# Two-branch mixer on one core: the first weight load split 1 to 3, x blocks loaded ahead of the q and k weights, one weight load held back, and new orders on all engines

## The chip, the core and the metric

One core of a Trainium2 chip runs the whole program. The metric is the device time of one execution in microseconds (us). The core has five engines that matter here: TensorE (PE, matrix products into PSUM banks), VectorE (DVE), ScalarE (ACT), GpSimd (POOL) and SyncE (SP). SP, ACT and POOL also issue DMAs, each in its own order; the DMAs all run on the same 16 DMA engines.

## What is computed

x has 2048 tokens of width 512, all data is bf16. xn is the layer norm of x (no gain or bias). Two branches work on xn, and the result is x + A + B.

```python
# A: 32 heads of 16; each token attends to itself and 7 earlier tokens, 2 apart
q, k, v = split(xn @ wqkv)
logits[s, w] = q[s] . k[s - 2*w] * 16**-0.5          # w = 0..7; before token 0: -1e9
A = (sum_w softmax(logits)[s, w] * v[s - 2*w]) @ wo
# B: gated MLP with mixing over tokens
z = gelu(xn @ w_in)                                   # 1792 columns: z1 | z2, 896 each
g = w_sp @ layernorm(z2) + b_sp                       # w_sp is 2048 x 2048
B = (z1 * g) @ w_out
```

## The kernel before

The program is first recorded as a list of named tasks, each with its engine, what it reads and writes, and (for a DMA) a channel. `Plan.add` (line 54) derives from that what each task waits for. `ORDERS` (line 206) then lists, written out by hand for each engine, the names of its tasks; `Plan.follow` (line 95) sets that order, and `Plan.emit` (line 117) writes each engine's instructions with the semaphore waits that the list of dependences asks for. Nothing reorders at run time: an engine that waits at a task holds all tasks listed behind it, SP's and POOL's DMA issues among them. So a task's place in `ORDERS` is as much a part of the kernel as what it does.

The 2048 tokens are 16 blocks of 128, in four groups of four. For block b the head of the program runs:

- `ldx{b}` (`ld_x`, line 525): the load of 128 KB of x into one of eight slots (slot b mod 8). x0, x1, x2 and x4 to x15 are issued by SP, x3 by ACT. A load into a slot used before waits until the block that had it has been normalised: x13 for norm5, x14 for norm6.
- `bnst`, `bnag` (DVE, lines 593 and 596): mean and variance; `rstd` (POOL, line 598): variance to the power of -0.5; `norm` (DVE, line 600): xn.
- The transpose to xnT. Blocks 0 to 3: `xTr` on PE (line 617), copied out of PSUM by `xTe` (ACT) and, for half of block 0, `xTf` (DVE). Blocks 4 to 15: `xTd`, a DMA transpose that SP issues (line 604).

Then PE makes, per block, `z2_{b}_0` and `z2_{b}_1` (`z_pair`, line 789; four matmuls of 448 columns each, PE line 799), `V{b}` (`v_pair`, line 637; four of 512 columns, PE line 644), and per group of four blocks `Q{j}_{c}` and `K{j}_{c}`, c = 0 to 3 (`qk_pair`, line 659; PE line 667). ACT takes them out of PSUM (`z2g`, `Ve`, `QKe`, `halo`). DVE forms the products of q and k for the logits (`prod`, line 692, and `padd`, line 696, 128 x 4096 elements each), PE sums them over a head (`lg`, line 705). V goes to a scratch tensor in DRAM (`Vw`, line 655) and is read back shifted. Later come the softmax, the `z1` products (needed from the end of the head on), the token mixing (`P1` to `P7`, PE line 922, with sums of w_sp and of z2 prepared by DVE), the gate and the output products (`out`, lines 1029 and 1033).

The weights of the head: `w_in2a` and `w_in2b` are the two 448-column halves of the z2 part of w_in, in four row chunks of 128. `ld_win_h` (line 535) loads each in two pieces of two chunks (224 KB each), the first issued by SP, the second by ACT. `ldq` and `ldk` (line 549, 512 KB each), `ldwv` (line 557, 512 KB) and `ldw_in1` (the z1 weights, 896 KB, line 531) are issued by SP. q, k and x4 to x7 wait for SP's piece of `w_in2a`:

```python
                512 * 512 * 2, ("wqk", which), reads=[("w_in2a", 0)],
...
        for b in range(4, 8):
            ld_x(b, "sp", after=[("w_in2a", 0)])
...
            if j == 1:
                ld_win("w_in1", 0, FH, "sp", after=[("xn", 2)])
```

SP's order begins `ldx0 ldx1 ldw_in2a_0 ldw_in2b_0 ldx2 ldx4 ldx5 ldq ldk ldx6 ldx7 ldx8 ldx10 ldx9 ldx11 ldw_in1 ldwv ldx12 xTd5 xTd7 ldx15 ldx14 xTd4`. DVE's order takes bnst5, 4, 7, 8 first after the statistics of blocks 0 to 3. POOL's order has the store `Vzero` (16 rows of zeros into the scratch tensor) behind rstd6.

Of the kernel before, what the change touches and what calls it, by code (L numbers as in the profile page):

```python
# [207 lines left out]
warm xTr0 fill0 z2_0_0 xTr1 z2_0_1 z2_1_0 xTr2 z2_1_1 xTr3 z2_2_0 z2_2_1 z2_3_0 Q0_0 z2_3_1 K0_0 K0_1 Q0_2 Q0_1
K0_2 K0_3 V0 V2 Q0_3 V1 V3 V4 V5 V7 Q1_0 K1_0 Q1_1 V6 Q1_3 K1_1 K1_3 K1_2 z2_4_0 Q1_2 z2_6_1 z2_4_1 z2_5_1
z2_5_0 z2_6_0 z2_7_1 z2_7_0 lg0_0 V11 V8 V9 V10 K2_0 K2_1 Q2_0 K2_2 Q2_1 Q2_2 K2_3 z2_8_1 Q2_3 z2_8_0 z2_9_0  # L210
z2_9_1 z2_10_0 z2_11_0 z2_11_1 lg1_0 z2_10_1 V13 V12 Q3_0 K3_0 Q3_1 V15 K3_1 V14 Q3_3 K3_3 z2_12_0 Q3_2 K3_2
z2_14_1 z2_12_1 z2_13_1 lg2_0 z2_13_0 z2_15_1 z2_15_0 z2_14_0 z1_0_0 z1_4_1 z1_0_1 z1_4_0 z1_2_0 z1_6_0 z1_10_0
z1_2_1 z1_10_1 z1_6_1 z1_8_1 z1_15_0 z1_15_1 z1_8_0 z1_12_1 z1_12_0 lg3_0 z1_9_1 z1_14_1 z1_9_0 z1_14_0 z1_13_0
z1_3_0 z1_13_1 z1_11_1 z1_11_0 z1_3_1 z1_7_1 z1_5_0 z1_5_1 z1_7_0 P1_0 z1_1_0 z1_1_1 P2_0 P5_0 P1_1 P6_0 P5_1
P3_0 P7_0 P6_1 P4_0 P2_1 P7_1 P1_2 P3_1 P4_1 P2_2 P1_3 P6_2 P5_2 P7_2 P3_2 P2_3 P5_3 P4_2 P6_3 out2_0 P7_3
out0_0 P1_4 P4_3 P3_3 P2_4 P6_4 P5_4 P7_4 out6_0 P1_5 P4_4 P3_4 P5_5 out4_0 out10_0 P2_5 P1_6 out8_0 P6_5 P5_6
P7_5 P3_5 P6_6 P4_5 out14_0 out12_0 P7_6 P2_6 P1_7 P3_6 out15_0 P4_6 P2_7 P6_7 out13_0 P7_7 P5_7 out11_0 P3_7
# [20 lines left out]
bnst4 bnst7 bnag4 bnst8 bnag8 bnst9 bnag7 bnag9 bnst10 bnst6 bnst11 norm4 bnag11 bnag6 norm5 norm7 prod0_0
bnag10 norm6 prod0_1 bnst12 zq0 norm11 prod0_2 padd0_1 bnag12 bnst15 norm10 norm8 bnst14 padd0_2 norm9 bnag15
bnag14 prod0_3 prod1_1 padd0_3 zv0 bnst13 norm15 prod1_0 norm14 prod1_2 bnag13 norm12 padd1_1 padd1_2 prod1_3  # L240
norm13 padd1_3 prod2_0 zq1 prod2_1 zv1 padd2_1 prod2_2 prod2_3 zq2 padd2_2 padd2_3 prod3_1 zv2 zn0 prod3_0
# [4 lines left out]
pvc2 sz3_1 srec1 pv14 u_8 pv12 S4_4 S13_5 pva2048_3 S2_5 pva1024_3 sattn1 h_4 pvc3 u_12 pv13 S4_5 S13_6 pv15
pva2048_4 u_15 pva1024_4 S2_6 pvc4 pv11 h_5 pv9 pva2048_5 S4_6 pva1024_5 S13_7 pvc5 pv5 S2_7 pv7 u_11 pva2048_6
h_6 pva1024_6 S4_7 pvc6 u_7 pv1 pv3 pva2048_7 pva1024_7 h_7 pvc7 u_1 u_3 fin1_1
""".split(),
    pool="""  # L250
ident0 mhalf rstd0 ident1 rstd1 rstd2 rstd3 ktpad mask0 mlog0 rstd5 mask1 rstd4 mlog1 rstd7 mlog2 rstd6 Vzero
rstd11 rstd10 rstd8 rstd9 rstd15 rstd12 rstd14 rstd13 zr0 zr1 ldbsp zr2 zr3 ldwo0 ldwo1 ldwout ldwo2 ldwo3
""".split(),
# [23 lines left out]
def build_kernel(nc, A_x, A_wqkv, A_wo, B_x, B_w_in, B_w_sp, B_b_sp, B_w_out, out,   # L277
# [82 lines left out]
    with ExitStack() as es:  # L360
# [164 lines left out]
        def ld_x(b, eng="sp", after=()):  # L525
            sl = b % 8
            dma(eng, lambda e: e.dma_start(xin_ap(sl), x2[128 * b:128 * b + 128, :]), 128 * 512 * 2,  # L527
                ("xin", sl), reads=after, writes=[("xin", sl)], name="ldx%d" % b)
# [650 lines left out]
```

## Time and profile before

| what | value |
|---|---|
| median of three runs | 228.82 us (228.8 to 229.11) |
| the profiled execution | 228.85 us, of it the span 227.1 us |
| granted TensorE clock | 1.0 |
| PE busy in the span | 97% |
| DVE busy in the span | 91% |
| ACT, POOL busy | 61%, 18% |

The span is the time from the first to the last instruction that the profile shows; the execution's own time has 1.75 us around it. A busy share of 97% says that there are some 6 us in which PE does nothing; where these lie, and what ends them, is asked of the waits and of the stretches. DVE is nearly as full, so that a gap on PE can also come from it.

### The profile page before, as it was taken

What the parts mean: (1) busy time and instruction counts of PE and PEld (TensorE: products, weight loads), DVE (VectorE), ACT (ScalarE), POOL (GpSimd) and SP (SyncE); (2) the same over time, 40 slices, a digit from 0 to 9 for tenths busy, and PEclk for the clock granted to TensorE, in tenths of its full rate; (3) what the DMA queues carried; (4) which work ended last, traced back from release to release, by engine and by line L of the source; (5) the groups of instructions that cost most, each with busy time, mean ns of one, the idle gap of its engine ahead of it and who ended that gap; (6) DMA issues with size and microseconds to landing.
All of it is one profiled execution on the core that took longest, in us unless ns stands there. A gap on an engine that the chain in (4) does not pass through costs nothing.

```text
span 227.1 us, 3077 instructions
## 1 busy us (share of the span) xinstructions
PE 220.9 (97%) x1142; PEld 115.6 (51%) x1142; DVE 207.3 (91%) x213; ACT 138.0 (61%) x247; POOL 39.9 (18%) x40
## 2 busy tenths in 40 slices
PE   7899799999999999999999999999999999999995
PEld 2454355455454676765555554454544544444443
DVE  4759999999999999999999999999999999999800
ACT  2579657988997898548547354345352546255651
POOL 2527929181320200201410000000000000000000
PEclk9999999999999999999999999999999999999999
DMA  6895464122964006855949669993899576378562
GB/s 204 258 360 130 116 179 102 26 69 45 222 172 118 0 0 208 99 111 136 248 123 213 139 169 227 192 226 73 170 197 211 156 157 140 115 156 179 155 150 69
DMA packets 84768, 34.18 MB, mean 151 GB/s; under 512 B 69281, under 2 KB 84401, under 8 KB 84753
## 3 DMA queue, kind: packets, MB, share of 16 engines
q1 hardware_dynamic: 74592, 23.90, 49.4%
q10 hardware_dynamic: 9280, 8.62, 13.2%
q0 software_dynamic: 880, 1.47, 2.1%
q8 instruction: 9, 0.15, 0.3%
q14 instruction: 7, 0.05, 0.1%
HBM read 12.98 MB, written 4.21 MB: 76 GB/s over the span
## 4 chain that ended last, share of the span: by engine, by line
PE 88%; DMA 5%; DVE 3%; SPq 2%; issue 0%; DVEq 0%
PE ps L922 37%; PE ps L799 19%; PE ps L1033 11%; PE ps L667 9%; PE ps L1029 6%; PE ps L644 5%; DMA arena<-in_A_x_dram 2%; DMA arena<-in_B_w_in_dram 2%; DVE fpool L593 2%; SPq L527 1%; DMA arena<-arena 1%; DVE arena L692 1%; PE ps L705 1%; DVE arena L600 0%; SPq L549 0%
## 5 line engine op out<-in xcount | busy, mean ns | idle before, releaser
L922 PE MATMUL ps<-arena 128*128 128x448 bf16 x448 | 86.5, 352 | 0.0
L922 PEld LDWEIGHTS ps<-arena 128*128 128x128 bf16 x448 | 43.8, 98 | 41.3
L799 PE MATMUL ps<-arena 128*128 128x448 bf16 x256 | 51.1, 353 | 0.5 <-DMA arena<-in_B_w_in_dram 0.5
L799 PEld LDWEIGHTS ps<-arena 128*128 128x128 bf16 x256 | 30.4, 121 | 18.9 <-issue 0.8
L992 DVE TENSOR_TENSOR arena<-arena 128x4096 bf16<-128x4096 bf16 x16 | 36.3, 2281 | 0.3
L692 DVE TENSOR_TENSOR arena<-arena 128x4096 bf16<-128x4096 bf16 x16 | 36.3, 2283 | 0.1
L810 ACT ACTIVATE arena<-ps 128x896 bf16<-128x896 f32 x32 | 28.4, 914 | 10.8 <-PE ps L799 10.8
L928 ACT ACTIVATE arena<-ps 128x448 bf16<-128x448 f32 x32 | 17.2, 540 | 25.7 <-PE ps L922 22.4
L667 PE MATMUL ps<-arena 128*128 128x512 bf16 x128 | 29.6, 379 | 0.0
L996 DVE TENSOR_TENSOR arena<-arena 128x4096 bf16<-128x4096 bf16 (+1 forms) x16 | 28.0, 1753 | 0.2
L598 POOL TENSOR_TENSOR fpool<-fpool 128x1 f32<-128x1 f32 x16 | 24.2, 1527 | 21.9 <-DVE fpool L596 21.9
L696 DVE TENSOR_TENSOR arena<-arena 128x4096 bf16<-128x4096 bf16 x12 | 27.4, 2286 | 0.1
L1033 PE MATMUL ps<-arena 128*128 128x512 bf16 (+2 forms) x119 | 27.0, 366 | 0.0
L667 PEld LDWEIGHTS ps<-arena 128*128 128x128 bf16 x128 | 14.5, 113 | 13.0
L675 ACT ACTIVATE arena<-ps 128x1024 bf16<-128x1024 f32 x16 | 16.1, 1027 | 6.1 <-PE ps L667 6.1
L1033 PEld LDWEIGHTS ps<-arena 128*128 128x128 bf16 x119 | 11.4, 98 | 12.8
L1042 ACT ACTIVATE arena<-ps 128x512 bf16<-128x512 f32 (+1 forms) x16 | 9.3, 589 | 13.1 <-PE ps L1033 12.9
L928 ACT ACTIVATE arena<-ps,fpool 128x448 bf16<-128x448 f32 x16 | 10.0, 630 | 11.8 <-PE ps L922 11.8
L644 PE MATMUL ps<-arena 128*128 128x512 bf16 x64 | 15.1, 379 | 1.6 <-DMA arena<-arena 1.6
L1029 PE MATMUL ps<-arena 128*128 128x512 bf16 (+2 forms) x68 | 16.6, 366 | 0.0
L818 ACT ACTIVATE arena<-arena 128x896 bf16<-128x896 bf16 x16 | 15.4, 960 | 0.1
L835 POOL TENSOR_TENSOR fpool<-fpool 128x4 f32<-128x4 f32 x4 | 9.0, 2258 | 33.8 <-DVE fpool L832 33.8
(71 smaller groups left out, 179.3 us busy)
## 6 DMA issues: line engine op xcount, KB each, us to landing
arena<-in_A_x_dram ACTq DMA_DIRECT2D x17, 128.0 KB, 2.4
vscr<-arena SPq DMA_DIRECT2D x16, 128.0 KB, 1.9
arena<-in_A_x_dram SPq DMA_DIRECT2D x15, 128.0 KB, 3.2
out_dram<-arena ACTq DMA_DIRECT2D x15, 128.0 KB, 2.2
arena<-in_A_wqkv_dram SPq DMA_DIRECT2D x3, 512.0 KB, 5.3
arena<-vscr ACTq DMA_DIRECT2D x6, 256.0 KB, 3.4
arena<-vscr ACTq DMA_DIRECT2D x1, 1152.0 KB, 6.2
arena<-vscr ACTq DMA_DIRECT2D x1, 1024.0 KB, 7.1
```

Source lines behind the costliest of these rows:

```text
L644: last = t.matmul(bank(k + i), AC(off["xnT"] + dc * S + 128 * (b + i), [[1, 128]]), AC(off["wv_raw"] + 512 * dc, [[1, 512]]), start=(dc == ...
L667: last = t.matmul(bank(k + which), AC(off["wqk"] + 1024 * dc + col0, [[4, 128]]), AC(off["xnT"] + dc * S + 512 * j, [[1, 512]]), start=(dc ...
L692: T("dve", lambda v: v.tensor_tensor(pbv, qb, kb, ALU.mult), reads=[("QT", c, j), ("KT", c, j), ("KTpad", c, j)], writes=[("pb", s_)], est ...
L696: T("dve", lambda v: v.tensor_tensor(A("pb", 4096, 4096 * a), A("pb", 4096, 4096 * a), A("pb", 4096, 4096 * b), ALU.add), reads=[("pb", b) ...
L799: last = t.matmul(bank(k + hf, HF), AC(off["xnT"] + dc * S + t0, [[ts, 128]]), AC(off["w_in"] + 1792 * dc + c0, [[1, HF]]), start=(dc == 0 ...
L810: T("act", lambda a: a.activation(A(nm, FH, FH * b).rearrange("p (t n) -> p t n", t=2), PC(512 * k, [[512, 2], [1, HF]]), ACTF.Gelu_apprx_ ...
L922: last = t.matmul(bank(k, HF), AC(lo + 128 * s, [[1, 128]]), mov(s), start=(first and s == 0), stop=(s == 7), skip_group_check=True)
L928: T("act", lambda a: a.activation(dst, bank(k, HF), ACTF.Identity, **kw), reads=[("ps", k), "bspf"], writes=[key], est=est, name="%s_%d" % ...
L992: T("dve", (lambda iv, tv, av: lambda v: v.tensor_tensor(tv, iv, av, ALU.mult))(iv, tv, av), reads=[("attn", pairs[i][b]) for b in blks] + ...
L996: T("dve", (lambda n: lambda v: v.tensor_tensor(AC(off["Vs"], [[4096, 2], [1, n]]), AC(off["Vs"], [[4096, 2], [1, n]]), AC(off["Vs"] + n, ...
L1029: t.matmul(po, AC(off["OT"] + 512 * os_ + 128 * cc, [[1, 128]]), AC(off["wo"] + 512 * cc + c0, [[1, n]]), start=False, stop=False, skip_gr ...
L1033: last = t.matmul(po, AC(off["uT"] + FH * us + 128 * fc, [[1, 128]]), AC(off["w_out"] + 512 * fc + c0, [[1, n]]), start=False, stop=(fc == ...
```

## The change

Four things are changed in the text of the kernel:

1. `ld_win_h` gets the place of its cut: `w_in2a` is dealt 1 chunk to SP (112 KB) and 3 to ACT (336 KB); `w_in2b` stays 2 and 2.
2. q, k and x4 to x7 wait for x1 and no longer for SP's piece of `w_in2a`. In SP's order x4, x5, x8, x6 and x7 stand ahead of q and k; `ldwv` now stands behind x10, x11, x9 and x13.
3. `w_in1` waits for the transpose of block 7, and stands behind `xTd11` in SP's order.
4. All five orders are new. The number and kind of instructions stay the same.

```diff
-        for nm, lo, hi, h0, h1 in (("w_in1", 0, FH, 0, 4), (("w_in2a", 0), FH, FH + HF, 0, 2),
-                                   (("w_in2a", 1), FH, FH + HF, 2, 4), (("w_in2b", 0), FH + HF, 2 * FH, 0, 2),
+        for nm, lo, hi, h0, h1 in (("w_in1", 0, FH, 0, 4), (("w_in2a", 0), FH, FH + HF, 0, 1),
+                                   (("w_in2a", 1), FH, FH + HF, 1, 4), (("w_in2b", 0), FH + HF, 2 * FH, 0, 2),
...
-        def ld_win_h(nm, lo, n):
-            for h in range(2):
+        def ld_win_h(nm, lo, n, cut):
+            for h, (c0, c1) in enumerate(((0, cut), (cut, 4))):
...
-        ld_win_h("w_in2a", FH, HF)
-        ld_win_h("w_in2b", FH + HF, HF)
+        ld_win_h("w_in2a", FH, HF, 1)
+        ld_win_h("w_in2b", FH + HF, HF, 2)
...
-                512 * 512 * 2, ("wqk", which), reads=[("w_in2a", 0)],
+                512 * 512 * 2, ("wqk", which), reads=[("xin", 1)],
...
-            ld_x(b, "sp", after=[("w_in2a", 0)])
+            ld_x(b, "sp", after=[("xin", 1)])
...
-            if j == 1:
-                ld_win("w_in1", 0, FH, "sp", after=[("xn", 2)])
             for b in bl:
                 ln_block(b)
+            if j == 1:
+                ld_win("w_in1", 0, FH, "sp", after=[("xnT", 7)])
```

The orders, as far as they belong to the head (the first tasks of each; the rest is permuted as well):

```diff
 pe:
-... z2_2_0 z2_2_1 z2_3_0 Q0_0 z2_3_1 K0_0 K0_1 Q0_2 Q0_1
-K0_2 K0_3 V0 V2 Q0_3 V1 V3 V4 V5 V7 Q1_0 K1_0 Q1_1 V6
+... z2_2_0 z2_2_1 z2_3_0 Q0_0 K0_0 K0_1 z2_3_1 Q0_1 Q0_3
+Q0_2 K0_2 V0 K0_3 V1 V3 V2 V7 V6 V4 K1_0 Q1_0 V5 Q1_1
 dve:
-... norm2 bnst5 norm3 bnag5 bnst4 bnst7 bnag4 bnst8 bnag8 bnst9 bnag7 bnag9 bnst10 bnst6 bnst11 norm4
-bnag11 bnag6 norm5 norm7 prod0_0 bnag10 norm6 prod0_1
+... norm2 bnst5 norm3 bnag5 bnst8 bnst7 bnst6 bnag6 bnst4 bnag7 bnag8 bnag4 bnst10 bnst11 norm5 bnst9
+norm6 prod0_0 norm7 bnst13 bnag10 bnag9 prod0_1 bnag13 zq0 norm4 padd0_1
 pool:
-ident0 mhalf rstd0 ident1 rstd1 rstd2 rstd3 ktpad mask0 mlog0 rstd5 mask1 rstd4 mlog1 rstd7 mlog2 rstd6 Vzero
-rstd11 rstd10 rstd8 rstd9
+ktpad ident0 mhalf Vzero ident1 rstd0 rstd1 rstd2 rstd3 rstd5 mask0 mlog0 mask1 mlog1 mlog2 rstd6 rstd7 rstd4
+rstd10 rstd9 rstd8 rstd15
 sp:
-ldx0 ldx1 ldw_in2a_0 ldw_in2b_0 ldx2 ldx4 ldx5 ldq ldk ldx6 ldx7 ldx8 ldx10 ldx9 ldx11 ldw_in1 ldwv ldx12 xTd5
-xTd7 ldx15 ldx14 xTd4 Vw0 xTd6
+ldx0 ldx1 ldw_in2a_0 ldw_in2b_0 ldx2 ldx4 ldx5 ldx8 ldx6 ldx7 ldq ldk ldx10 ldx11 ldx9 ldx13 ldwv ldx14 xTd5
+xTd6 xTd7 ldx15 xTd4 Vw1 Vw3 ldx12
```

More of the change, by code (lines that the diff above doesn't have):

```diff
@@ L207 @@
     pe="""
[L208 to L217, printed above, removed]
@@ L218 @@
-P4_7 out9_0 out7_0 out5_0 out3_0 out1_0 out1_1
+warm xTr0 fill0 z2_0_0 xTr1 z2_0_1 z2_1_0 xTr2 z2_1_1 xTr3 z2_2_0 z2_2_1 z2_3_0 Q0_0 K0_0 K0_1 z2_3_1 Q0_1 Q0_3
+Q0_2 K0_2 V0 K0_3 V1 V3 V2 V7 V6 V4 K1_0 Q1_0 V5 Q1_1 Q1_3 K1_1 Q1_2 K1_2 z2_4_1 z2_4_0 z2_5_0 K1_3 z2_7_0
+z2_5_1 z2_6_0 z2_6_1 z2_7_1 V9 V10 V8 lg0_0 Q2_0 K2_1 K2_0 V11 Q2_1 Q2_2 K2_3 K2_2 Q2_3 z2_8_1 z2_8_0 z2_9_0
+z2_10_1 z2_9_1 z2_10_0 z2_11_0 z2_11_1 lg1_0 V15 V12 V14 V13 K3_2 Q3_1 K3_1 Q3_2 K3_0 Q3_0 z2_13_0 z2_13_1
+z2_12_0 K3_3 z2_12_1 z1_0_0 Q3_3 lg2_0 z2_15_0 z1_0_1 z2_15_1 z2_14_1 z2_14_0 z1_4_0 z1_4_1 z1_6_1 z1_2_0 z1_6_0
@@ L237 @@
 steps0 steps1 zeros bnst0 bnag0 norm0 bnst1 bnag1 xTf0 norm1 bnst2 bnag2 bnst3 bnag3 norm2 bnst5 norm3 bnag5
[L238 to L241, printed above, removed]
@@ L247 @@
-pva2048_4 u_15 pva1024_4 S2_6 pvc4 pv11 h_5 pv9 pva2048_5 S4_6 pva1024_5 S13_7 pvc5 pv5 S2_7 pv7 u_11 pva2048_6
-h_6 pva1024_6 S4_7 pvc6 u_7 pv1 pv3 pva2048_7 pva1024_7 h_7 pvc7 u_1 u_3 fin1_1
+bnst8 bnst7 bnst6 bnag6 bnst4 bnag7 bnag8 bnag4 bnst10 bnst11 norm5 bnst9 norm6 prod0_0 norm7 bnst13 bnag10
+bnag9 prod0_1 bnag13 zq0 norm4 padd0_1 bnst15 norm10 prod0_2 bnag15 bnag11 norm9 padd0_2 bnst12 bnst14 prod0_3
+norm8 bnag14 norm11 padd0_3 prod1_0 zv0 bnag12 prod1_1 norm15 padd1_1 prod1_2 norm12 prod1_3 padd1_2 zq1 norm14
@@ L249 @@
+sattn1 u_8 S4_4 pva1024_2 S13_5 pvc2 S2_5 pv14 u_12 pv12 pva2048_3 S4_5 h_4 pva1024_3 pvc3 pv15 pv13 S13_6
+pva2048_4 S2_6 pva1024_4 h_5 S4_6 pvc4 pv11 u_15 pv9 S13_7 pva2048_5 pva1024_5 h_6 pvc5 u_11 pv5 S2_7 pv7
+pva2048_6 pva1024_6 pvc6 u_7 pv3 S4_7 pv1 pva2048_7 pva1024_7 h_7 pvc7 u_3 u_1 fin1_1
 """.split(),
     pool="""
-ident0 mhalf rstd0 ident1 rstd1 rstd2 rstd3 ktpad mask0 mlog0 rstd5 mask1 rstd4 mlog1 rstd7 mlog2 rstd6 Vzero
-rstd11 rstd10 rstd8 rstd9 rstd15 rstd12 rstd14 rstd13 zr0 zr1 ldbsp zr2 zr3 ldwo0 ldwo1 ldwout ldwo2 ldwo3
+ktpad ident0 mhalf Vzero ident1 rstd0 rstd1 rstd2 rstd3 rstd5 mask0 mlog0 mask1 mlog1 mlog2 rstd6 rstd7 rstd4
@@ L253 @@
+rstd10 rstd9 rstd8 rstd15 rstd11 rstd14 rstd12 rstd13 zr0 zr1 ldbsp zr2 zr3 ldwout ldwo0 ldwo1 ldwo2 ldwo3
 """.split(),
     sp="""
-ldx0 ldx1 ldw_in2a_0 ldw_in2b_0 ldx2 ldx4 ldx5 ldq ldk ldx6 ldx7 ldx8 ldx10 ldx9 ldx11 ldw_in1 ldwv ldx12 xTd5
-xTd7 ldx15 ldx14 xTd4 Vw0 xTd6 Vw2 Vw1 Vw4 Vw3 xTd10 ldx13 Vw5 xTd8 xTd9 xTd11 Vw7 Vw6 xTd15 xTd12 Vw8 xTd14
-xTd13 wT1_1 Vw9 Vw11 wT0_1 wT1_0 Vw13 Vw10 Vw15 Vw12 wT0_0 Vw14 lgT2 lgT0 lgT3 lgT1 wT2_0 wT2_1 wT3_0 wT3_1 OTd0
-uT_2 uT_0 uT_4 wT4_0 wT4_1 wT5_0 OTd1 uT_6 wT5_1 OTd2 uT_8 uT_10 wT6_0 wT6_1 OTd3 uT_12 uT_14 uT_13 wT7_0 wT7_1
@@ L259 @@
-OTd4 uT_15 uT_11 OTd5 OTd6 uT_9 uT_5 uT_7 OTd7 uT_3 uT_1 st1_0
+ldx0 ldx1 ldw_in2a_0 ldw_in2b_0 ldx2 ldx4 ldx5 ldx8 ldx6 ldx7 ldq ldk ldx10 ldx11 ldx9 ldx13 ldwv ldx14 xTd5
+xTd6 xTd7 ldx15 xTd4 Vw1 Vw3 ldx12 Vw0 Vw2 xTd9 Vw6 xTd8 Vw4 xTd10 Vw5 xTd11 ldw_in1 xTd15 Vw7 Vw9 xTd12 wT1_1
+xTd14 Vw8 xTd13 Vw11 Vw10 wT0_0 Vw14 wT0_1 Vw12 wT1_0 Vw15 Vw13 lgT0 lgT2 lgT1 lgT3 wT2_0 wT3_0 wT2_1 wT3_1
+wT4_0 OTd0 uT_0 uT_2 wT4_1 wT5_0 uT_4 OTd1 uT_6 wT5_1 wT6_0 uT_12 uT_10 uT_8 OTd2 wT6_1 wT7_0 wT7_1 uT_14 OTd3
@@ L260 @@
+uT_15 uT_13 OTd4 OTd5 uT_11 uT_9 uT_5 OTd6 uT_7 OTd7 uT_3 uT_1 st1_0
 """.split(),
```

53 lines of the change are left out of this document (30 added, 23 removed).

## The prediction

> **What bounds the kernel now.** I read the engine table first, then the stretches, then the waits, then the chain that ended last. The first two say which engine sets the end and where it is not full:
>
> ```profile
> PE 220.9 (97%) x1142; PEld 115.6 (51%) x1142; DVE 207.3 (91%) x213; ACT 138.0 (61%) x247; POOL 39.9 (18%) x40
> ```
>
> ```profile
> core 0: us, PE busy (x) PEld busy (x) DVE busy (x) ACT busy (x) POOL busy (x), PEclk, DMA share, GB/s
> ...
> 12.00:18.00 6.00, 6.00 (x31) 3.14 (x30) 4.32 (x11) 4.26 (x10) 1.46 (x4) 1.00 1.04 352
> 18.00:24.20 6.20, 6.18 (x29) 2.79 (x27) 6.20 (x11) 6.02 (x13) 5.82 (x5) 1.00 0.53 111
> 24.20:25.80 1.60, 0.05 (x1) 0.05 (x2) 1.60 (x4) 0.82 (x2) 1.60 (x2) 1.00 0.64 156
> 25.80:60.00 34.20, 34.20 (x177) 16.78 (x178) 34.06 (x30) 26.55 (x53) 16.26 (x6) 1.00 0.40 98
> ```
>
> Columns: stretch, length, then busy us of each engine. PE is full from 12 us on, except 24.20 to 25.80; from 25.8 to 224.8 it never waits, at granted clock 1.00. The change alters no matmul, so 199 us behind 25.8 are fixed unless an edit opens a gap there, and all that can be won are the gaps ahead. The waits name them:
>
> ```profile
> DVE fpool L593 <- DMA arena<-in_A_x_dram: 4.7, 3, 2.7
> ...
> PE ps L644 <- DMA arena<-arena: 1.6, 1, 1.6
> ```
>
> L644 is the V product; it waits once, 1.6 us, for the DMA transpose of a block (V4 for xnT 4). L593 is bn_stats; its longest wait, 2.7 us, is for an x block. The chain joins the two:
>
> ```profile
> 1.73 4.47 DMA arena<-in_B_w_in_dram
> 6.20 0.02 issue
> 6.22 0.34 SPq L527
> ...
> 8.65 4.97 DMA arena<-in_A_x_dram
> 13.62 0.02 issue
> 13.65 0.69 DVE fpool L593
> ...
> 23.15 2.56 DMA arena<-arena
> 25.71 0.04 issue
> 25.75 2.76 PE ps L644 x12
> ```
>
> First number: start. The SP half of the first z2 weights lands at 6.20; until then SP may not issue x4. Block 7, behind the 1 MB of q and k weights, lands at 13.62, and DVE, which takes it as its next block, stands still from 10.95. Everything behind it on DVE is late by that, down to norm6 (ends 21.48). SP's load of x14 waits for norm6, and the transpose of block 4 stands behind that load: issued at 23.15, landed at 25.71, V4 at 25.75.
>
> **The stall's size.** The V product before V4 starts at 23.16. Start to start a product of four 512-column matmuls takes 0.863, so V4 could start at 24.02: the stall is 25.75 - 24.02 = **1.73 us**.
>
> **The change, part by part.**
>
> *z2 weights 1 to 3.* SP's piece becomes 112 KB, ACT's 336 KB. In the trace ACT's half landed at 4.48, SP's at 6.20, though issued only 0.64 apart: in 2 to 6 us each queue moved some 170 KB/us, and SP had x0 and x1 in front. Now 368 KB (SP) stand against 336 KB (ACT), so both should be in by about 5.5 (estimate: at 170 KB/us each, with the 0.9 us from last packet to landing that the 6.20 shows). z2_0_0 started at 6.35; its other operands were ready at 5.96 (ACT's copy of block 0) and 6.10 (DVE's), so at most 0.15 is won there. It is not kept: PE next waits at 9.42 (0.31 of idle) for the transpose of block 2, set by norm2 (ends 9.37) and so by x2's landing at 7.33. x2 comes when nearly all 1408 KB of the head loads are through, which the dealing does not change. I take 0; the other bound is -0.31, if SP's 112 KB less bring x2 in 0.65 earlier. The Trainium skill, "DMA: Bandwidth & Descriptors", section "Issuing engines are not separate DMA queues", says that DMAs of all issuers interleave on the same 16 engines and that issuing from several saves only sequencer time. By it this edit is worth nothing (227.1); by the queue rates of the trace up to 0.3 (226.8).
>
> *x4 to x8 ahead of q and k, waiting for x1 and not for w_in2a.* x1 landed at 4.46, so SP issues x4 at 4.5 (was 6.22), then x5, x8, x6, x7 at steps of 0.47, q at 6.85 and k at 7.35 (were 7.08 and 7.55). The queue is then never empty. Blocks 6 to 11 landed 0.37 apart (128 KB, 346 KB/us); from x2's 7.33 that gives x7 at 9.2 (was 13.62), q at 10.7, k at 12.3. Upper bound: q's and k's old landings, 11.03 and 12.88, plus 384 KB more in front (1.1): 12.1 and 14.0. PE needs q at 12.90 (Q0_0) and k at 13.76 (K0_0): no cost, at the bound 0.24.
>
> *DVE's order.* Steps from the trace: bn_stats 0.60, bn_aggr 0.10, norm 0.31, a product 2.20. From 10.30 (end of bnag5's turn): bnst8, 7, 6, bnag6, bnst4, three bnag, to 13.1; bnst10, bnst11 to 14.3; norm5 ends at 14.7; bnst9; norm6 ends at 15.6; prod0_0 (was 18.80) to 17.8; norm7 ends at 18.2; bnst13, two bnag; prod0_1 18.9 to 21.1; bnag13, zq0; norm4 ends at 21.75. Against before: norm5 is 3.9 earlier, norm6 5.9, norm7 0.7, norm4 3.65 *later*. POOL's rstd 6, 7, 4 fall at 12.2 to 14.1, under no product, where one takes 0.56; under products they took 1.9 to 4.9 (rstd11, rstd9). The 2.7 us of DVE idle are filled.
>
> *SP's order.* x13 needs norm5: issued at 14.75; wv at 15.25 (was 11.50); x14 at 15.75 (needs norm6); transposes 5 and 6 at 16.2 and 17.5, 7 at 18.75, x15, 4 at 21.8. A transpose landed 2.4 to 3.3 after issue, the first one 4.2. So xnT 7 at 22.0 or before, xnT 6 likewise, xnT 4 at 21.8 + 2.56 = 24.4.
>
> *PE's order.* From z2_2_0 at 10.63 to V0 there are the same 12 products as before, so V0 stands at 19.70 again; then K0_3, V1, V3, V2, and V7 at 24.02, V6 24.88, V4 25.74, K1_0 (all four blocks) 26.6. Spare: V7 2.0, V4 1.3. Even a transpose as slow as the slowest (4.2) costs V4 only 0.3. **The stall goes: -1.73.** Next late is wv: with q's latency (3.95; q too had only x blocks in front, as wv has x13) it lands at 19.2, half a us ahead of V0. Its own old latency, behind the 896 KB of w_in1, was 7.50. I take 3.95: w_in1 is gone from in front.
>
> *z1 weights held for xnT 7.* Their load goes behind the transpose of block 11, near 37 to 40 us; it took 6.62. z1_0_0 stands near 70, and the stretch moves 98 GB/s where 352 was seen. Cost 0; the cover is over 20 us. xTd15 and two V stores stand behind it on SP; the wait is long satisfied, so they lose only its 0.43 of issue. The load of w_in1 out of the head is what lets wv come late.
>
> *POOL.* The Vzero store (0.70 of POOL at 18.92, ahead of rstd11) goes to about 1.4, ahead of ident1 (0.28) and rstd0, whose input comes at 3.86: nothing waits, and rstd11 and later lose a neighbour. 0.
>
> *Orders behind 26 us.* The same products, activations and DVE passes are permuted. DVE had 34.06 of 34.20 us busy and 39.7 of 40, so it is as full as PE and could open gaps; but it starts its products 3 us sooner. I laid the new orders out with the durations of these rows and found no PE wait over 0.2 us; margins of 0.2 to 0.5 us against ACT's evictions are common in both orders, and before, none of them became a gap. Cost 0, with up to +1.0 as the far bound (the longest single PE wait in the trace but the one removed is 0.5, twice that).
>
> **Sum.** The profiled execution took 228.85 (span 227.1, so 1.75 around it), the median is 228.82: the same. 228.85 - 1.73 = **227.1**; span 225.4.
>
> **Rivals.**
>
> 1. *wv takes the stall's place, slower than before.* wv is issued 3.75 us later because x13, in front of it, waits for norm5, and norm5 for x10 and x11. If it needs its old 7.50 it lands at 22.75, V0 waits 3.05, and the time is 227.1 + 3.05 = **230.2**. It decides once wv lands after 19.70 + 1.73 = 21.4. For: half a us of margin, in-order SP, 512 KB. Against: by 15 us the queue has drained, and no other bulk load is in front.
> 2. *Part of the gain is given back.* q and k at their upper bounds put x10 and x11 at 14.4 and 14.8; norm5 ends near 15.9, wv lands near 20.4, V0 is 0.7 late; or waits on ACT or DVE behind 26 us add as much. **227.8**, up to 228.4. For: every second margin is under 0.5. Against: k would have to be slower than the old rate.
> 3. *It does not do what it says.* x4 to x8 enter a queue still full with head loads; if they land no earlier than before (x7 at 13), DVE stands still as before and the new order, with norm4 behind two products, has V4 waiting again: **about 228.8**. Against: 13 would need under 120 KB/us, and 338 was seen from 11 to 19 us.
> 4. *The head gains too*: x2 earlier by the lighter SP queue: **226.8**.
>
> **How the numbers follow.** Forecast 227.1 (226.9 to 227.5): 0.54. Rival 4: 0.10. Rival 2: 0.16, of it 0.02 within 0.2%. Rival 3: 0.05, all of it same. Rival 1: 0.15, all slower. About 0.2%, 0.46 us, is what a measurement of this kernel can tell from no change: below 228.4 is faster, above 229.3 slower. Faster 0.54 + 0.10 + 0.14 = 0.78, same 0.07, slower 0.15. The range leaves out rival 1, and rival 3 half: 226.7 to 228.7.
>
> **What would show it.** Right: bn_stats no longer waits 2.7 us for x; x4's issue near 4.5; no wait of L644 for a transpose; prod0_0 near 15.6; PE full from 10 us on; span near 225.4. Wrong: a wait of L644 for A_wqkv (rival 1); bn_stats waiting for x10 or x11 (rival 2); bn_stats still waiting for x7 (rival 3); any PE wait over 0.3 us behind 26 us, named by its releaser (ACT: an eviction; DVE: a product or sum), would refute the nought for the orders.

## The result: slower by 0.9%

| | before | after |
|---|---|---|
| median | 228.81 us (228.80 to 229.11, 4 runs) | 230.71 us (230.66 to 231.30, 4 runs) |
| after / before, 95% interval | | 1.0086 [1.0068, 1.0104] |
| profiled execution, of it the span | 228.85, 227.1 us | 230.73, 229.0 us |
| granted clock | 1.0 | 1.0 |

Forecast were 227.1 us and a range of 226.7 to 228.7: wrong by 3.6 us, and on the other side. The experiments below ran later, on three chips, on which the kernel before spread over 227.6 to 232.8 us where it had spread by 0.3 here; so they are read as ratios to the kernel before run beside them, from which executions at a lower clock or over 1.5% above the fastest of their kernel are left out, and the profile of an experiment is one execution out of 4 to 12.

### The profile page after: what moved, and what is told of

Same layout as the page of the kernel before. It is cut to its first block, busy times and chain, and to the rows that moved or that the text cites. A ratio compares the mean times of both kernels' runs of the same rounds, so it can differ in the third digit from the quotient of the medians.

```text
span 229.0 us, 3069 instructions
## 1 busy us (share of the span) xinstructions
PE 221.9 (97%) x1129; PEld 115.2 (50%) x1142; DVE 208.5 (91%) x213; ACT 137.8 (60%) x247; POOL 40.4 (18%) x40
## 4 chain that ended last, share of the span: by engine, by line
PE 63%; DVE 18%; DMA 13%; issue 3%; SPq 1%; DVEq 0%; ACT 0%
PE ps L800 19%; PE ps L923 17%; PE ps L668 9%; PE ps L1034 7%; PE ps L645 6%; DVE arena L997 5%; DMA arena<-in_A_x_dram 4%; PE ps L1030 4%; DVE arena L993 4%; DMA arena<-in_B_w_sp_dram 3%; DVE arena L895 2%; DMA arena<-vscr 2%; DMA arena<-in_A_wqkv_dram 2%; DMA arena<-arena 2%; DVE arena L955 1%
## 5 line engine op out<-in xcount | busy, mean ns | idle before, releaser
L923 PE MATMUL ps<-arena 128*128 128x448 bf16 x448 | 86.6, 353 | 1.0 <-ACT arena L929 0.6
L923 PEld LDWEIGHTS ps<-arena 128*128 128x128 bf16 x448 | 43.5, 98 | 43.2 <-ACT arena L929 1.1
L929 ACT ACTIVATE arena<-ps 128x448 bf16<-128x448 f32 x32 | 16.9, 541 | 35.1 <-PE ps L923 22.2
L811 ACT ACTIVATE arena<-ps 128x896 bf16<-128x896 f32 x32 | 28.6, 916 | 9.1 <-PE ps L800 8.9
L668 PE MATMUL ps<-arena 128*128 128x512 bf16 x124 | 28.9, 380 | 0.8 <-ACT arena L811 0.4
L1034 PE MATMUL ps<-arena 128*128 128x512 bf16 (+2 forms) x117 | 26.7, 367 | 0.1
L599 POOL TENSOR_TENSOR fpool<-fpool 128x1 f32<-128x1 f32 x16 | 21.5, 1357 | 20.2 <-DVE fpool L597 20.0
L668 PEld LDWEIGHTS ps<-arena 128*128 128x128 bf16 x128 | 14.3, 114 | 14.1 <-issue 1.0
L1034 PEld LDWEIGHTS ps<-arena 128*128 128x128 bf16 x119 | 11.4, 98 | 12.9
L836 POOL TENSOR_TENSOR fpool<-fpool 128x4 f32<-128x4 f32 x4 | 12.3, 3064 | 30.9 <-DVE fpool L833 30.9
L1030 PE MATMUL ps<-arena 128*128 128x512 bf16 (+2 forms) x63 | 15.5, 366 | 0.7 <-DMA arena<-arena 0.4
L645 PE MATMUL ps<-arena 128*128 128x512 bf16 x62 | 14.5, 380 | 0.5 <-DMA arena<-in_A_wqkv_dram 0.3
L929 ACT ACTIVATE arena<-ps,fpool 128x448 bf16<-128x448 f32 x16 | 10.0, 628 | 7.1 <-PE ps L923 7.1
```

Source lines behind the costliest of these rows:

```text
L645: last = t.matmul(bank(k + i), AC(off["xnT"] + dc * S + 128 * (b + i), [[1, 128]]), AC(off["wv_raw"] + 512 * dc, [[1, 512]]), start=(dc == ...
L668: last = t.matmul(bank(k + which), AC(off["wqk"] + 1024 * dc + col0, [[4, 128]]), AC(off["xnT"] + dc * S + 512 * j, [[1, 512]]), start=(dc ...
L811: T("act", lambda a: a.activation(A(nm, FH, FH * b).rearrange("p (t n) -> p t n", t=2), PC(512 * k, [[512, 2], [1, HF]]), ACTF.Gelu_apprx_ ...
L923: last = t.matmul(bank(k, HF), AC(lo + 128 * s, [[1, 128]]), mov(s), start=(first and s == 0), stop=(s == 7), skip_group_check=True)
L929: T("act", lambda a: a.activation(dst, bank(k, HF), ACTF.Identity, **kw), reads=[("ps", k), "bspf"], writes=[key], est=est, name="%s_%d" % ...
L1030: t.matmul(po, AC(off["OT"] + 512 * os_ + 128 * cc, [[1, 128]]), AC(off["wo"] + 512 * cc + c0, [[1, n]]), start=False, stop=False, skip_gr ...
```

## The profile after

Where PE stands still now, in the table by stretches of the changed kernel (columns as in the forecast: length, then busy us of each engine, granted clock, DMA share, GB/s):

```profile
12.00:18.00 6.00, 5.38 (x26) 2.62 (x26) 4.18 (x12) 4.07 (x8) 1.69 (x4) 1.00 0.31 101
18.00:24.20 6.20, 5.92 (x28) 2.71 (x27) 6.20 (x10) 4.82 (x13) 3.31 (x2) 1.00 0.98 185
24.20:25.80 1.60, 1.55 (x8) 0.77 (x8) 1.60 (x2) 1.41 (x5) 1.60 (x1) 1.00 0.56 136
25.80:60.00 34.20, 33.94 (x175) 16.73 (x177) 34.08 (x31) 27.19 (x54) 14.91 (x8) 1.00 0.50 132
60.00:102.00 42.00, 41.95 (x226) 26.86 (x225) 41.86 (x46) 33.79 (x55) 10.14 (x5) 1.00 0.49 110
102.00:226.00 124.00, 122.16 (x618) 60.27 (x623) 112.40 (x96) 60.84 (x108) 3.67 (x5) 1.00 0.76 159
```

The same view of the kernel before, for the last two:

```profile
60.00:102.00 42.00, 42.00 (x226) 26.52 (x224) 41.74 (x45) 32.28 (x53) 6.79 (x4) 1.00 0.49 106
102.00:224.00 122.00, 122.00 (x625) 61.27 (x624) 112.33 (x98) 62.29 (x109) 3.87 (x5) 1.00 0.76 166
```

The 1.55 us hole at 24.2 is gone, as forecast. Two others stand in its place: 0.9 us between 12 and 24.2, and 1.84 us behind 102, where PE had been full. A bookkeeping of PE's products shows the same two places: start of each product (of its first weight load) minus the start of the one before it and its usual pitch (V, Q, K 0.863, z 0.757, P 1.513, out 2.375), summed up. By 30 us the kernel before has lost 2.65, the changed one 2.16; at 102 us it is 3.13 and 2.66; at the end 3.16 and 5.03. So the head won 0.49, and the stretch behind 102 us lost 2.37 where it had lost 0.03: 228.85 - 0.49 + 0.02 (from 30 to 102 us) + 2.34 = 230.72, the profiled time to 0.01. Of the 3.6 us by which the forecast was off, the head makes 1.2 and the stretch behind 102 us the rest. A weight load starts up to 0.2 us ahead of its first matmul, so a single wait counted at the weight load, as those below are, can be 0.2 more than PE loses by it.

The waits name the releasers (us in all, times, longest):

```profile
DVE fpool L594 <- DMA arena<-in_A_x_dram: 3.7, 3, 1.7
...
DVE arena L895 <- DMA arena<-in_B_w_sp_dram: 2.3, 1, 2.3
...
PEld ps L923 <- ACT arena L929: 1.1, 1, 1.1
...
PEld ps L923 <- DVE arena L895: 0.8, 1, 0.8
...
PEld ps L645 <- DMA arena<-in_A_wqkv_dram: 0.8, 1, 0.8
PEld ps L668 <- DMA arena<-in_A_wqkv_dram: 0.7, 1, 0.7
...
PEld ps L923 <- DVE arena L898: 0.5, 1, 0.5
PEld ps L1030 <- DMA arena<-arena: 0.5, 1, 0.5
```

bn_stats (L594) no longer stands 2.7 us for block 7, but 1.7 for block 10. L645 (V0) and L668 (K0_0) wait for their weights; so does Q0_0, which began at 13.24, just behind q's landing at 13.14. Behind 102 us L895 is `S13_2`, DVE's first sum of the transposed w_sp of pair 2; before, no wait of it over 0.2 us is in this view. PE's P products (L923) then wait for DVE's sums (L895, L898) and for an eviction (L929): P6_2 0.42 us, P5_5 0.71, P7_5 0.94. The eviction in turn overwrites what DVE's sum `h_4` reads, and began at 170.86, just behind the end of `h_4` at 170.77. L1030, an output product, waits for a DMA transpose (out12_0 for `OTd3`, 0.76), and out3_0 for `uT_3` 0.39. Counted at the matmuls the five lose 0.23, 0.53, 0.76, 0.60 and 0.17, together 2.29 of the 2.34.

The chain that ended last, from 100 to 132 us. Before, it was PE alone:

```profile
102.04 1.51 PE ps L799 x8
103.55 28.57 PE ps L922 x151
```

After, it leaves PE for the second transpose of pair 2, `wT2_1`, and goes on over DVE:

```profile
101.57 15.74 PE ps L923 x84
117.31 7.92 DMA arena<-in_B_w_sp_dram
...
125.32 1.22 DVE arena L895
126.55 1.14 DVE arena L997
```

PE's share of the whole chain fell from 88% to 63%, DVE's rose from 3% to 18%, that of DMA from 5% to 13%. Issued at 117.31, `wT2_1` landed at 125.23; before, issued at 117.20, it landed at 123.20. Two things differ beside it. On SP `wT3_0` stands ahead of `wT2_1` now, and three of these transposes are issued within 6.6 us. And ACT issues `ldV0_9`, 256 KB of V read back for DVE's `pv` products, at 119.78 (landed 124.96) and not at 104.61 (108.92). The trace keeps sixteen marks of completion for every load: of `wT2_1`'s, twelve came by 124.06 and the last four at 124.47 to 125.23; before, all sixteen came within 0.1 us.

## The experiments

Names as in the orders; "new" marks an edit of the changed kernel or its orders, "old" one of the kernel before.

### Which part loses: head and rest joined crosswise

Four kernels join the first part of one kernel's orders (106 tasks of PE, 116 of DVE, 57 of SP, 31 of POOL, and what of ACT belongs to them) to the rest of the other's.

```diff
 e1_newhead_oldrest    new head, old rest
 e2_oldhead_newrest    old head, new rest
 e5_newhead_oldrest2   as e1, the three early V loads (ldV0_0, _11, _13) where the new orders have them
 e6_oldhead_newrest2   as e2, ldV0_0 where the old orders have it, ldV0_13 and ldV0_11 behind ldxr0
```

> The changed kernel, but with the orders of the kernel before from the token mixing on (PE behind lg3, DVE behind the first softmax maximum, SP behind the logit transposes, POOL behind zr3; ACT's tasks of that stage). Theory A (two parts: the new head wins about 0.5 us, the new orders behind it lose about 2.4): 228.3 to 228.5, no PE wait over 0.3 us behind 102 us. Rival B (the loss behind 102 us comes from what the new head leaves behind, such as other landing times, and not from the order there): 230 to 231.

> The kernel before, but with the changed kernel's orders from the same cuts on (all loads and weights' dealing as before). Theory A: the loss alone, 228.8 + 2.4 = 231.2, with DVE's first sum of w_sp rows for pair 2 again standing about 2 us for the transpose of w_sp. Rival B: about 228.8.

Measured: e1 1.0041 [1.0008, 1.0073], e2 1.0239 [1.0177, 1.0301]. e1's median, 230.21, lies in rival B's range, but the kernel before, run beside it, stood at 229.19, so that the loss is 0.4% and lies between the theories; e2 fits neither. The seam has a part in both. In e1 the 1152 KB load `ldV0_0` fell beside the first two of SP's four transposes for the softmax, and DVE waited for one:

```profile
DVE arena L766 <- DMA arena<-arena: 2.6, 1, 2.6
```

Those two took 6.5 and 7.2 us, the other two 4.3 and 3.7; before, all four took 3.2 to 4.6. In e2 three V loads fell beside them. What e1 does tell: the DMA transposes beside a bulk load came late.

> As e1, but the three early V loads (1152, 256 and 256 KB) stand where the changed kernel has them, well ahead of the logit transposes; in e1 the largest ran beside these transposes, which then landed in up to 7.2 us instead of 3 to 5, and DVE stood 2.56 us. If that collision is what e1 lost: DVE does not wait at the softmax maximum, and the time is 228.0 to 228.6 (theory A). If the new head itself leads to the loss behind it: 229.5 or more, as e1.

> As e2, but the 1152 KB V load stands where the kernel before has it and the two others behind the first x reloads, so that none runs beside the logit transposes. Theory A (the new orders of the later stage cost about 2.4 us by themselves): 230.5 to 231.5. Rival B (they cost nothing; the loss needs the new head): 228.5 to 229.3.

Measured: e5 1.0036 [1.0004, 1.0067], e6 1.0141 [1.0083, 1.02]. In e5's execution no PE wait over 0.3 us is left behind 102 us and 1.4 us are won in the head, but z1_9_1 and z1_14_1 wait 0.53 and 0.97 us for evictions, since PE's z1 products and ACT's gates come from different lists at the seam. e5 lies between its theories. e6 loses, as theory A says, by more than it says. The split speaks for the rest of the orders as the loser, but every kernel has a seam of its own.

```diff
 e10_newhead_split     new up to and with the z1 products, their gates and the early V loads; old from P on
```

> The changed kernel up to and with its z1 products, z1 gates and the early V loads, joined to the old orders from the P products on (PE's P and out products, DVE's sums behind the softmax, ACT's last stretch with the old place of the late V load, SP's and POOL's last transposes). Theory A (the loss sits in the orders behind 102 us): no wait of DVE for a w_sp transpose over 0.5 us, no PE wait over 0.4 us behind 102 us, time 227.5 to 228.6. Rival (the head's landings cost it, or the loss comes back anywhere): 229.5 or more.

Measured: 1.0015 [0.9989, 1.0042], median 228.98, between the two. Its profiled execution has no DVE wait for w_sp in its list and one new wait at the seam (P2_0, 0.97 us). Its time of 230.1 comes from that wait and from the head, where q landed at 14.08.

### The late w_sp transpose: its place on SP

```diff
 e3_wT2_swap (new, SP)
-... wT2_0 wT3_0 wT2_1 wT3_1
+... wT2_0 wT2_1 wT3_0 wT3_1
```

> The changed kernel, with one task moved on SP: the second w_sp transpose of pair 2 (wT2_1) ahead of the first one of pair 3 (wT3_0), as it was before. Theory C (one cause behind 102 us: this transpose lands 2.3 us late for DVE, and the later PE waits follow from it): DVE's 2.3 us of idle go, time 228.4 to 229.0. Rival D (the later waits for S13_5, for h_4 and for the transpose OTd3 have causes of their own in the order): only 0.3 to 0.5 are won, 230.2 to 230.5.

Measured: 1.0095 [1.0046, 1.0143]. Theory C's remedy failed. In the waits of this kernel:

```profile
PEld ps L923 <- DMA arena<-in_B_w_sp_dram: 4.0, 1, 4.0
PE ps L923 <- DMA arena<-in_B_w_sp_dram: 3.6, 1, 3.6
```

`wT3_0`, now behind `wT2_1`, took 8.73 us, and PE's P1_3, which reads it, waited. This execution, 235.2 us at a granted clock of 0.985, is longer than most of the kernel's, so its sizes are not carried over; the ratio does not rest on it.

### The late V load, taken away and put in

```diff
 e12_ldV_early (new, ACT)
-ldxr2 ldxr0 S5_0 ... g12_0 g21_0 ldV0_9
+ldxr2 ldxr0 ldV0_9 S5_0 ... g12_0 g21_0
 e14_before_late_ldV (old, ACT)
-... sexp0 ldV0_9 fk_1 ... S2e_1 S3e_1 g11_1
+... sexp0 fk_1 ... S2e_1 S3e_1 ldV0_9 g11_1
```

> The changed kernel with one edit: the last 256 KB load of the V columns (block 9 on) is issued on ACT right behind the first two reloads of x and so some 10 us earlier, as it was in the kernel before, and not while SP's transposes of w_sp are in flight. Theory A (the late transpose of w_sp is slow because of the loads beside it): it lands near 123.3, DVE idles under 0.5 us for it, the waits of P6_2, P5_5 and P7_5 shrink, time 228.5 to 229.5. Rival (its place behind another transpose on SP alone makes it late, or the waits of PE behind it have their own causes in the orders): DVE still idles over 1.2 us for it, or the time stays 230.2 or more.

> The kernel before with one edit: the 256 KB load of the V columns from block 9 on is issued by ACT some 15 us later, at about 120 us as in the changed kernel, while SP's transposes of w_sp are in flight. Theory A (the load beside them makes the transpose late): the second w_sp transpose of group 2, 6.0 us from issue to landing before, takes 7.5 to 10, DVE waits 1 to 3 us for it at S13_2, and the time is 0.3 to 2 us over the kernel before of the same chip, 229.0 to 230.7. Rival (the swapped order of the transposes on SP makes it late, the load does not): under 7 us, DVE waits under 0.5 us, the time within 0.3 us of the kernel before.

Measured: e12 0.9998 [0.9963, 1.0032]; e14 1.0075 [1.0034, 1.0117]. One load moved by 18.7 us, and the changed kernel takes as long as the kernel before; the same load moved by 15.6 us puts a loss of 0.75% into the kernel before. e12's waits:

```profile
DVE arena L895 <- DMA arena<-in_B_w_sp_dram: 1.0, 1, 1.0
...
PE ps L1030 <- DMA arena<-arena: 0.8, 1, 0.8
```

`wT2_1` took 6.77 us and DVE waited 0.97, not 2.26; P6_2 and P5_5 wait no more, P7_5 0.44. So the new order of the transposes costs DVE something by itself, against "under 0.5". Nor is all of the loss gone: by the bookkeeping, PE still loses 1.42 us behind 102 us in this execution, most of it at out12_0 (1.15, for `OTd3`, which the new order puts behind both transposes of group 7 on SP). Its 228.41 comes out because the head, with q at 11.53, wins 1.86. Against the changed kernel's profile the stretch behind 102 us is thus better by 0.95 us, and the head by the other 1.4. In e14 the load (issued 120.2, landed 126.3) did not delay `wT2_1` (6.1 us), as theory A had it, but the next transpose, and the chain goes through that:

```profile
103.52 15.83 PE ps L922 x84
119.36 7.18 DMA arena<-in_B_w_sp_dram
...
126.58 5.47 PE ps L922 x28
```

Before, this transpose took 5.56; P1_3 waits 0.71 here. Behind 102 us PE loses 0.92, where it had lost 0.03. The profiled execution, 229.71, is among e14's fastest (229.3 to 237.3); where the slower ones lose more was not seen.

### Is the loss the kernel's own? And the version with both loads early

```diff
 e8_after_again, e15_after_third   the changed kernel
 e4_wv_early (new, SP)
-... ldx11 ldx9 ldx13 ldwv ldx14
+... ldx11 ldx9 ldwv ldx13 ldx14
 e13_ldV_and_wv_early, e19_both_again   e12 and e4 together
```

> The changed kernel once more, unchanged, beside the other three, for a second profile of it: whether its waits for S13_2 (DVE, for a w_sp transpose), for wv and for k come again. Theory A: 230.4 to 231, the same places. If they are chance landings of single DMAs: other places, 228 to 231.

> The changed kernel again, on the chip and in the call of the next three, so that all stand against the same runs of the kernel before. If the loss is the kernel's own: 230.0 to 231.0, DVE waiting over 1.2 us for the second w_sp transpose of group 2. If it was one of the first chip's: within 0.5 us of the kernel before.

> The changed kernel, with one task moved on SP: the load of wv ahead of that of x13, so that it no longer stands behind norm5. In the changed kernel V0 waits 0.65 us for wv. If PE's lost time adds up to the end: wv lands near 19.0, the wait goes, 230.1. If DVE sets the pace of the later stage: the wait goes and the time stays at 230.6 to 230.7.

> The kernel of the run with the V load early, and the V weights' load ahead of that of x block 13 on SP, so that it does not wait for norm5. If both the head's wait for the V weights (0.65 to 0.76 us in the changed kernel) and the collision behind 102 us are taken away, the time is 227.5 to 228.7. If the loss sits in the order of PE, DVE or ACT behind 102 us itself, 229.5 to 230.7.

> The kernel of the run with the V load and the V weights early again, beside the one with q moved: 227.6 to 228.3, 0.4 to 1.1 us under the kernel before of the same chip, if its gain is its own; within 0.3 us of the kernel before if it was chance.

Measured: e8 1.0023 [0.998, 1.0067], which leaves it open; e15 1.0089 [1.0052, 1.0127], the first ratio again. The waits came again in both profiles: `wT2_1` took 11.18 us in e8 and 9.49 in e15, with `ldV0_9` in flight beside it, DVE waited 4.9 and 3.5 us for it, and V0 0.76 and 0.62 for the V weights. e4 0.9988 [0.9941, 1.0035], with a gap in its times: 227.4 to 228.5 four times, 230.2 to 231.7 eight times. Over all their executions the medians of e4 and e8 are 230.61 and 231.06, with the kernel before at 229.19 and 228.89, so that the two ratios flatter them. In e4's profiled execution, 227.79, V0 does not wait (the V weights landed at 18.2), DVE waits 1.2 us for `wT2_1`, and PE loses 2.10 us in all. So the forecast time can be had with the late V load in place, but not as a rule. Executions over 230 us: with the load late (after, e4, e8, e15) 26 of 35; with it early (e12, e13, e16, e18, e19) 9 of 60; the kernel before in all experiments 27 of 138. Some of these kernels have other edits too, and they ran at different times; e15 and e16 (1.0089 and 0.9977) ran side by side.

e13 0.9979 [0.9948, 1.0009]; e19, the same kernel on the same chip later, 1.0023 [0.999, 1.0055]: its gain is not shown. In e13's profiled execution (227.49) q landed at 11.5 and PE lost 1.81 us in all; in e19's (230.40) q landed at 13.57, Q0_0 and K0_0 waited 0.82 and 0.42, and behind 150 us P7_5, out12_0 and out1_0 0.84, 0.75 and 0.72.

### One more transpose moved

```diff
 e16_both_OTd3 (e13, SP)
-... wT6_1 wT7_0 wT7_1 uT_14 OTd3
+... wT6_1 OTd3 wT7_0 wT7_1 uT_14
```

> The changed kernel with three moves: the late V load early on ACT, the V weights ahead of x block 13 on SP, and the transpose of O rows 3 (OTd3) ahead of the w_sp transposes of group 7 on SP, since out12_0 waited 0.76 to 1.33 us for it behind them. If that wait was only its place: no wait of out12_0, 227.2 to 227.9. If moving it ahead makes the transposes of group 7 late, or only hands the wait on (to the products of group 7 or to out3_0): 228.2 or more.

Measured: 0.9977 [0.9949, 1.0006], median 228.25: no better than e13. No wait of out12_0 was left, but its profiled execution was the slowest of its twelve (232.41), so the trace does not tell what the move is worth. It tells something else:

```profile
DVE arena L895 <- DMA arena<-in_B_w_sp_dram: 2.7, 1, 2.7
```

`wT2_1` took 8.35 us with the late V load gone, and P6_2, P5_5 and P7_5 waited 0.76, 0.70 and 0.94, as in the changed kernel. So these waits can come without that load; by the counts above, they come less often.

### The head: the stall by itself, the dealing by itself, q's place

```diff
 e7_xTd4_first (old, SP)
-... ldx12 xTd5 xTd7 ldx15 ldx14 xTd4 Vw0 xTd6 Vw2
+... ldx12 xTd4 xTd5 xTd7 ldx15 ldx14 xTd6 Vw0 Vw2
 e9_before_xTd4_first (old, SP)
+... ldx12 xTd4 xTd5 xTd7 ldx15 ldx14 Vw0 xTd6 Vw2
 e17_z2_dealing_alone   the kernel before with part 1 of the change (the cut of w_in2a at one chunk)
 e18_q_ahead_of_x7 (e13, SP)
-... ldx5 ldx8 ldx6 ldx7 ldq ldk ldx10
+... ldx5 ldx8 ldq ldx7 ldx6 ldk ldx10
```

> The kernel before with two tasks moved on SP and nothing else: the transpose of block 4 ahead of those of 5 and 7 (and so ahead of the loads of x15 and x14), that of block 6 ahead of the first V store. It removes V4's wait of 1.7 us by itself. If a PE wait of the head reaches the end one to one: 227.1. If the later stage is paced by DVE and by the landings of the w_sp transposes, which a PE that is ahead does not move: V4's wait goes and new waits behind 100 us take it back, 228.3 to 228.9.

> The kernel before, with one edit: the transpose of x block 4 stands ahead of those of blocks 5 and 7 on SP's list. All else, the z2 dealing, the x blocks, w_in1 and every order, is as before. It asks what the 1.73 us of V4 are worth by themselves. Theory A (a gap of PE taken out of the stretch ahead of 26 us reaches the end one to one): V4 has no wait of over 0.4 us, the time is 1.3 to 1.8 us under the kernel before of the same chip, 227.0 to 227.6. Theory B (what is won in the head is given back later, whatever the orders): V4's wait is gone and the time is within 0.5 us of the kernel before, 228.3 to 228.9, with a new wait of over 1 us in the transpose or z1 stretch.

e7: 1.01 [1.0033, 1.0168], by an edit that did more than was meant. `xTd6`, moved too, stood ahead of the store `Vw0`; ACT's Ve4 needs that store's buffer and came at 28.6 (26.8 before), Ve2 stands behind it, and Q1_0, which needs Ve2, waited 3.19 us. e9, without that: 0.9989 [0.9968, 1.0009]. V4 does not wait, but Q1_0 (0.57, for Ve2) and z2_6_1 (0.38) do; by 30 us PE has lost 1.36 us and not 2.65, at the end 2.37 and not 3.16. The profile lies between the theories, with some 0.8 us won of a stall of 1.73; the times fit theory B, with 0.25 us won (from 0.7 won to 0.2 lost), but the new wait of over 1 us behind it did not come. The kernel before keeps little spare behind the stall, so taking it out lets the next waits through.

> The kernel before with the z2 weights dealt 1 to 3 over the two queues and nothing else. By the nought taken for it: within 0.3 us of the kernel before, x2 landing at 7.2 to 7.4, V4 waiting 1.7 us. By the bound: x2 under 7.0 and 0.2 to 0.3 us faster. A third case, that ACT's larger piece comes later than SP's did: first z2 product at 6.5 or later, 0.2 us slower.

e17: 1.0017 [0.9988, 1.0046], in us from 0.3 won to 1.1 lost; x2 landed at 7.2 (before 7.33), V4 waited 1.42 and the first z2 product began at 6.55. No gain is seen, and the forecast's better bound of 0.31 is just outside the interval; nought and the third case, 0.2 us slower, are both inside. The Trainium skill, "DMA: Bandwidth & Descriptors", section "Issuing engines are not separate DMA queues", has DMAs of all issuers run on the same 16 engines, so that dealing saves only issue time; that no gain is seen agrees with it.

> The changed kernel with the late V load early on ACT and the V weights ahead of x block 13, and in the head the q weights ahead of x blocks 7 and 6 on SP (x blocks 4, 5, 8, then q, 7, 6, k). With q behind five x blocks its landing varied from 11.5 to 14.1 us in the runs so far, and Q0_0 needs it at 12.6; with q behind the x blocks 4 and 5 alone, in the kernel before, it varied from 10.7 to 11.4. Theory A (q's place in the queue is what varies): q lands by 11.2, Q0_0 has no wait, DVE waits under 0.5 us for blocks 7 and 6, 227.3 to 227.9. Rival (the queue is slow as a whole in some executions, and what is put behind q, that is blocks 7 and 6 and k, comes late in q's stead): a wait of DVE for block 7 or 6, or of K0_0 for k, of 0.5 us or more, and a time no better than the kernel of the next run.

e18: 0.9973 [0.9948, 0.9997], median 228.13 (forecast 227.3 to 227.9): theory A in the head (q landed at 10.5, Q0_0, K0_0 and blocks 6 and 7 without a wait), and the one kernel of the study with an interval under 1, by so little that chance is not excluded. What stands behind it is seen in the stretches of the changed kernel

```profile
12.00:13.00 1.00, 1.00 (x6) 0.39 (x4) 0.97 (x5) 0.98 (x3) 0.59 (x2) 1.00 0.84 293
13.00:14.00 1.00, 0.62 (x4) 0.37 (x4) 0.19 (x3) 1.00 (x3) 0.89 (x3) 1.00 0.19 65
14.00:15.00 1.00, 0.76 (x4) 0.26 (x3) 0.14 (x1) 0.33 (x2) 0.20 (x1) 1.00 0.06 20
```

and of e18:

```profile
12.00:13.00 1.00, 1.00 (x7) 0.49 (x5) 0.96 (x3) 0.98 (x3) 0.53 (x3) 1.00 0.78 263
13.00:14.00 1.00, 1.00 (x6) 0.56 (x5) 1.00 (x5) 1.00 (x3) 0.89 (x3) 1.00 0.03 9
14.00:15.00 1.00, 1.00 (x7) 0.51 (x5) 1.00 (x3) 0.59 (x2) 0.48 (x1) 1.00 0.65 163
```

In the changed kernel the share of the 16 DMA engines falls to 0.19 and 0.06 while q (13.14), k (14.50) and x10 (14.84) are still to land: nearly all bytes are through, a thin rest keeps three loads from being done, and SP's next loads wait for norm5 behind x10. In e18 nothing trails. The sixteen marks of each load show the rest: of q's, fourteen had come by 11.35, the last two at 12.47 and 13.14; of k's and x10's the last two trailed likewise (13.84 and 14.50; 14.19 and 14.84). In e18 q's sixteen lie between 9.84 and 10.46. In all twelve profiles with five x blocks ahead of q the eighth of q's marks came at 10.9 to 11.5, and the last at 11.5 to 14.1: what varies most is when the last parts are done, not the mean rate. Which engines lagged, and why, the marks do not tell. The Trainium skill, "DMA: Bandwidth & Descriptors", section "Why a DMA increments its semaphore by 16 and not by 1", says that a DMA's engines finish independently and that it counts as landed only when the last has; these marks agree with that.

## Why the forecast was wrong, point by point

- **The stall goes, -1.73: right as a mechanism.** V4 waits for no transpose in the changed kernel (`xTd4` landed at 26.08, V4 began at 26.79). Of the 1.73 the head kept 0.49. The "12 products" ahead of V0 in the forecast are 11, in both orders; its 19.70 comes out of 11.
- **z2 dealing 0: no gain, as forecast** (e17), though the two pieces landed at 5.89 and 5.01, not both by 5.5. **x blocks first: right** for x7 (9.18, forecast 9.2); x1 came at 4.85 and so x4 was issued at 4.86, not 4.5. **z1 weights held, 0: right**: issued at 40.5, landed at 45.4, z1_0_0 at 71.8. **POOL 0**: no wait of another engine for POOL has grown (L601 for L599 0.9 us, before 1.1).
- **q at 10.7 (bound 12.1), k at 12.3 (bound 14.0): wrong beyond the bounds.** 13.14 and 14.50 here, 11.5 to 14.1 for q in the other kernels with this head. The rate of 346 KB/us held for most of the bytes (the eighth of q's sixteen marks came at 10.97) and not for the last of them. Q0_0 and K0_0 waited 0.49 and 0.43 us, where 0 to 0.24 was allowed. The 338 KB/us that rival 3 cites for 11 to 19 us is 311 in the view of that stretch; nothing hangs on it.
- **wv lands at 19.2: its latency right (4.04 against 3.95), its issue wrong.** SP's wait for norm5, and DVE's 1.7 us for x10, put it at 16.87, not 15.25; V0 waits 0.65. These two points are rival 2 as it was written, at a higher price: counted at the matmuls, as the 1.73 is, Q0_0, K0_0 and V0 give back 0.33 + 0.41 + 0.44 = 1.18 of it, and the rest of the head some 0.06, which leaves the 0.49. The head alone would have made 228.36, the far end of rival 2. `prod0_0` began at 17.5, not 15.6.
- **"Orders behind 26 us. ... Cost 0, with up to +1.0 as the far bound": the step that failed.** It cost 2.34. The new orders were laid out with the durations of the rows before, and in those a w_sp transpose takes 6.0 us; but the orders themselves move `ldV0_9` beside the transposes, and `wT2_1` takes 7.92. DVE, which is free for `S13_2` at 123.06, waits 2.26 us, and P6_2, P5_5 and P7_5 lose 1.52 downstream; out12_0 and out3_0 lose the rest at DMA transposes of their own. e14 shows that the load alone makes such a loss, in the kernel before; that it is the larger part of the loss here rests on the times of e12 and on e16 against e15. It is not the whole: with it gone `wT2_1` takes 6.4 to 7.0 us in the new order of the transposes, DVE waits 0.6 to 1.4 (e12, e13, e18, e19), and PE still loses 0.5 to 2.1 behind 102 us in these four profiles (3.6 in e16's). e3 shows that putting the transposes back in their old order is no remedy by itself. The list of what would refute the nought did name it: a PE wait over 0.3 us behind 26 us, released by DVE or ACT.
- **Open:** why the changed kernel sits at 228 us in some of the later executions and at 231 in most, with the late load in all of them, and why e16's transposes were late without it; what each part of the new orders costs beside the load (`wT3_0`'s place on SP was moved only with the load late, `OTd3`'s only together with other moves); and what the rest of the gain of the head is worth once q's place is mended (e18 only shows 0.03 to 0.5%).

## What to carry to other kernels

When an order is changed, list for each engine's queue which transfers now overlap which, and do not carry a DMA's latency over from the old trace: ask first of all what bulk load now runs beside a transpose that somebody waits for. Behind a stall that is taken out, add up the spare of the next few consumers; here it was less than the stall. Where a load queue is reordered, a load that is put further back is done when the last of its parts is, not when the mean rate says so: keep the load with the least spare near the front.

## What the runs showed of the hardware

- DMA transposes beside bulk loads from the ACT queue. `wT2_1` (512 KB) took 6.0 us in the kernel before; in the new orders 7.2, 7.9, 9.5 and 11.2 with a 256 KB load in flight beside it (e4, the changed kernel, e15, e8; the last at a granted clock of 0.993), but 4.6 and 9.4 with that load in flight in e2 and e6 (new rest behind the old head), and 6.4 to 7.0 in four executions of the new orders, with 8.4 in a fifth (e16), without it. The next one took 5.6 in the kernel before, 7.2 with that load (e14). Those for the softmax took 3.2 to 4.6, and 6.5 and 7.2 beside a load of 1152 KB (e1).
- The landing of a 512 KB load behind five 128 KB loads came 11.5 to 14.1 us into the span in kernels with the same instructions ahead of it, though half of its sixteen marks came by 10.9 to 11.5 in all of them; where it stood three places further ahead it landed at 10.7 to 11.4.
- The first z2 products began at 6.16 to 6.69 us in kernels with the same head, at granted clock 1.00.
